# FFN of the second and third token group in triples of hidden units, and one output projection moved ahead

## The chip, the cores and the metric

The kernel runs on one core of one Trainium2 chip. The metric is the device time of one execution in microseconds (us). The engines of the core are named as in the profile: PE is TensorE's matrix multiplication and PEld its weight load, DVE is VectorE, ACT is ScalarE, POOL is GpSimd and SP is SyncE, which here only issues DMAs.

## The reference

The input `x` holds 2048 tokens of 640 values. They are normalized, and two branches work on the result: a local attention with 32 heads of 20 values, in which a token looks at 8 tokens two positions apart, with its own output projection `wo`; and a feed-forward network (FFN) with 1536 hidden values. The branches are multiplied and added to the input.

```
xn  = layernorm(x)
q, k, v = split(xn @ wqkv)                        # 640 -> 3 * 640, 32 heads of 20
s   = local_attention(q, k, v; offsets 0, 2, .. 14) @ wo
g   = silu(silu(xn @ w1) @ w2)                    # 640 -> 1536 -> 640
out = x + s * g
```

## The kernel before

**Groups.** The tokens are worked in four groups of 512: two halves of the sequence, each split by even and odd positions. The texts count them 1 to 4; in the code `g` runs from 0 to 3. A group's 512 tokens are four token tiles (`t`) of 128. Each group passes through a q/k/v stage (`qkv_phase`) and an FFN stage (`ffn_phase`). The attention of a group is computed on VectorE (`scores`, `values`) while TensorE goes on, so a group's output projection (`wo_phase`) comes a stage later: within the FFN stage of the next group. The last group's projection stands at the end (`wo_last`).

**Precision.** Every operand is kept as a high half and a low remainder, and a product is made as high times high, low times high and high times low. So each weight tile (`w`) has a high and a low part, the normalized input has `th` and `tl`, and a hidden unit has `sh` and `sl`.

**FFN units.** The 1536 hidden values are twelve units of 128. *Up* unit f (`up`, L1130 to L1132) makes 15 products of 512 columns into one of two PSUM banks called `rot`. ScalarE then takes silu of the bank twice: once into `sh` (L1143), once into the single buffer `sf` (L1144). VectorE subtracts the two and leaves the low half `sl` (L1145). There are three buffers each of `sh` and `sl`, used in turn. *Down* unit f (`down`, L1003 and L1005 by way of `tm_mm`) makes 16 products from `sh` and then 8 from `sl`, which add into six banks called `acc`: one of 384 columns for each token tile (list `a`) and one of 2 x 256 for each two tiles (list `b`). When all twelve are in, ScalarE takes silu of the sums into `gate` (L1219).

**The output projection.** `wo_phase` has five weight chunks with 24 products each (three for each of four token tiles and two column ranges), L1003 and L1005 again, from `th` and `tl` of the transposed attention output. It takes the same six `acc` banks. VectorE multiplies the sums into `gate` (L1035, six instructions), POOL adds the input (L1049), and SP stores the result. After it `gate` serves as a buffer for transposing the next group's input by DMA (`turn_x`).

**Banks.** `bank()` hands out the six `acc` banks in turn. The q/k/v stage takes four for each of its four quarters, the projection six and the FFN six. ScalarE evacuates the quarters (L733, L736, L739).

**Weights.** All units stand in a list `units` in the order in which TensorE needs them, which is derived from `plan(g)`. A ring of seven buffers `w` is filled seven units ahead: when a unit is done (`w_done`), `w_load` prepares the unit seven places on. Weights that were used before come as ready halves from device memory by a DMA that POOL issues (L564). Fresh ones come raw by a DMA that SP issues (L538), and are split by ScalarE (high half, L573) and VectorE (low half, L577). In group 2 the five chunks of `wo` are fresh, and the FFN units come as ready halves.

**Order.** TensorE's order is the order of the program. For the other engines a planner (`Weave`) lists the instructions with estimated durations and priorities and writes out an order for each queue before the program is built: each engine runs its queue in that order. Every change of TensorE's order therefore lets the planner write new orders for VectorE, ScalarE, POOL and SP. VectorE and POOL instructions marked `lock` are never planned at the same time.

`plan(g)` writes the order of the FFN stage. Before the change it is, for groups 2 to 4: up 0, the projection, and then pairs "up f, up f + 1, down f - 1, down f" (in the last group single units from the seventh on), and the remaining down unit at the end. Group 1 has no projection.

Of the kernel before, what the change touches and what calls it, by code (L numbers as in the profile page):

```python
# [18 lines left out]
DC, FC = D // P, F // P  # L19
# [4 lines left out]
T = 4  # L24
# [5 lines left out]
CA, CB = 384, 256  # L30
RING = 7
NS = 3
SINGLE = 6
RAW_AHEAD = 10
TURNS = 1
FIRST_AT = 44.0, 60.0
# [41 lines left out]
def tsl(t):  # L78
    return slice(t * P, (t + 1) * P)
# [7 lines left out]
class Weave:  # L87
# [22 lines left out]
    def add(self, eng, dur, fn, reads=(), writes=(), prio=0.0, lock=False, table=None, nbytes=0, more=0.0, late=0.0, at=0.0,  # L110
            spans=(), quick=False):
        o = Op()
        o.quick = quick
        o.eng, o.dur, o.fn, o.prio, o.lock, o.table, o.nbytes = eng, dur, fn, prio, lock, table, nbytes
        o.more, o.late, o.spans = more, late, spans
        o.seq, o.users, o.at, o.need = len(self.ops), [], at, 0
        before = set()
        for k in reads:
            if k in self.writer:
                before.add(self.writer[k])  # L120
        for k in writes:
            if k in self.writer:
                before.add(self.writer[k])
            before.update(self.readers.get(k, ()))
        for k in writes:
            self.writer[k] = o
            self.readers[k] = []
        for k in reads:
            self.readers.setdefault(k, []).append(o)
        before.discard(o)  # L130
        self.ops.append(o)
        for b in before:
            self.chain(b, o)
        return o
# [164 lines left out]
def local_attention_silu_ffn(ctx: ExitStack, tc: tile.TileContext, x, wqkv, wo, w1, w2, out):  # L299
# [9 lines left out]
    xg = x.rearrange("b (g p j) d -> (b g) p j d", p=P, j=J)  # L309
    og = out.rearrange("b (g p j) d -> (b g) p j d", p=P, j=J)  # L310
    OL_AT = {10: 2}
    groups = [(h, par) for h in range(2) for par in range(2)]
    NG = len(groups)

    def rows(view, g):
        h, par = groups[g]
        return view[h, :, par::2, :]
# [46 lines left out]
    def take(kind, n):  # L364
        i = count[kind] % n
        count[kind] += 1
        return i

    def bank():
        i = take("acc", 6)  # L370
        return ACC[i], ("acc", i)
# [11 lines left out]
    def dve(n, fn, reads, writes, prio, lock=False, late=0.0, spans=()):  # L383
        return add("DVE", dv(n), fn, reads, writes, prio, lock, late=late, spans=spans)
# [8 lines left out]
    def pe(dur, fn, reads, writes, spans=()):  # L393
        add("PE", dur, fn, reads, writes, spans=spans)
        clock[0] += dur

    def dma(fn, reads, writes, nbytes, prio, dur=0.45, more=0.0, quick=False):
        add("SP", dur, fn, reads, writes, prio, nbytes=nbytes, more=more, quick=quick)
# [15 lines left out]
    def plan(g):  # L414

        last = g == NG - 1
        todo = [("w1", 0)] + [("wo", 0)] * (g > 0)
        down = 0  # L420
        f = 1
        while f < FC:
            k = f // 2
            pair = f + 1 < FC and not (last and f > SINGLE)
            if g < TURNS and 1 <= k <= DC and k - 1 not in X_DMA:
                todo.append(("x", k - 1))
            if last and f in OL_AT:
                todo.append(("o", OL_AT[f]))
            if last and f == FC - 1:
                todo.append(("rest", (0, 1)))  # L430
            n = 2 if pair else 1
            todo += [("w1", u) for u in range(f, f + n)]
            f += n
            todo += [("w2", u) for u in range(down, down + n)]
            down += n
        return todo + [("w2", u) for u in range(down, FC)]

# [2 lines left out]
    for g in range(NG):  # L442
        units += [("q", q, c) for q in range(NQ) for c in range(DC)]
        for kind, f in plan(g):
            units += [("wo", c) for c in range(DC)] if kind == "wo" else [(kind, f)] if kind in ("w1", "w2") else []
# [27 lines left out]
    for u in units:  # L473
        n = seen[u] = seen.get(u, 0) + 1
# [118 lines left out]
    def w_next(*want):  # L593

        i = used[0]
        assert units[i] == want and i < loaded[0], (units[i], want)
        used[0] += 1
        s, n, at = i % RING, width(i), start(i)
        return WR[s][:, at:at + n], WR[s][:, D + at:D + at + n], ("wh", s), ("wl", s)

    def w_done(n=1):
        for _ in range(n):
            w_load()
# [380 lines left out]
    def t_keys(i, cs, ts=range(T), kinds=("th", "tl")):  # L984
        return [(k, i, c, t) for k in kinds for c in cs for t in ts]
# [8 lines left out]
    def tm_banks():  # L994
        a = [bank() for t in range(T)]
        b = [bank() for t in range(T // 2)]
        return a, b

    def tm_mm(banks, t, st, w, first, last, cols=(0, 1)):
        a, b = banks  # L1000
        h = t % 2
        if 0 in cols:
            nc.tensor.matmul(a[t][0][:, :CA], st, w[:, :CA], start=first, stop=last)  # L1003
        if 1 in cols:
            nc.tensor.matmul(b[t // 2][0][:, h * CB:(h + 1) * CB], st, w[:, CA:], start=first and h == 0,  # L1005
                             stop=last, skip_group_check=True)

    def tm_views(banks):

        a, b = banks  # L1010
        for k in range(T // 2):
            for t in (2 * k, 2 * k + 1):
                yield a[t][0][:, :CA].rearrange("p (t m) -> p t m", t=1), a[t][1], slice(t, t + 1), slice(0, CA)
            yield b[k][0].rearrange("p (t m) -> p t m", t=2), b[k][1], slice(2 * k, 2 * k + 2), slice(CA, D)

    def gkeys(ts, cs):
        return [("g", t, cs.start) for t in range(ts.start, ts.stop)]
# [1 line left out]
    TM = mm(CA) + mm(CB)  # L1019

    def wo_phase(g, i):
        banks = tm_banks()
        a, b = banks
        for c in range(DC):
            wh, wl, kh, kl = w_next("wo", c)
            for t in range(T):
                def one(c=c, t=t, wh=wh, wl=wl):
                    tm_mm(banks, t, OH[i][:, c, tsl(t)], wh, c == 0, False)
                    tm_mm(banks, t, OH[i][:, c, tsl(t)], wl, False, False)
                    tm_mm(banks, t, OL[i][:, c, tsl(t)], wh, False, c == DC - 1)  # L1030
                pe(3 * TM, one, t_keys(i, [c], [t]) + [kh, kl], [a[t][1], b[t // 2][1]])
            w_done()
        for p, kp, ts, cs in tm_views(banks):
            n = (ts.stop - ts.start) * (cs.stop - cs.start)
            dve(n, lambda p=p, ts=ts, cs=cs: nc.vector.tensor_tensor(  # L1035
                out=G[:, ts, cs], in0=p, in1=G[:, ts, cs], op=OP.mult), [kp], gkeys(ts, cs), 0, late=ADD_LATE)
        if g == NG - 2:
            for t in range(T):
                xr, kx = (XR[t], [("xr", t)]) if t < 3 else (PRV[:, :D], PRK)
                rest.append((t, xr, kx))  # L1040
                if t < 3:
                    dma(lambda t=t, xr=xr: nc.sync.dma_start(xr, rows(xg, g)[:, t, :]), [], kx, P * D * 4, clock[0] + 5)
            return
        add("DVE", HOLD, lambda: None, [("g", t, CA) for t in range(T)], ["hold"], 0)
        for t in range(T):
            s = take("xr", 3)
            xr = XR[s]
            dma(lambda t=t, xr=xr: nc.sync.dma_start(xr, rows(xg, g)[:, t, :]), [], [("xr", s)], P * D * 4, clock[0] + 5)
            add("POOL", po(D), lambda t=t, xr=xr: nc.gpsimd.tensor_tensor(out=xr, in0=xr, in1=G[:, t, :], op=OP.add),  # L1049
                [("g", t, 0), ("g", t, CA)], [("xr", s)], 500, lock=True)  # L1050
            dma(lambda t=t, xr=xr: nc.sync.dma_start(rows(og, g)[:, t, :], xr), [("xr", s)], [], P * D * 4, clock[0] + 20)
# [208 lines left out]
```

## Time and profile before

| | us |
|---|---|
| three timed runs | 624.53, 624.95, 624.99; median 624.95 |
| the profiled execution | 624.74 |
| its span (first to last instruction) | 623.0 |
| PE busy in it | 617.8 |
| DVE busy in it | 541.4 |
| ACT busy in it | 267.7 |
| POOL busy in it | 114.9 |

The profile shows one execution. Rows of a timeline give the start and the duration in us, then the engine, the line of the kernel, the operation and what it writes and reads; `SPq` is SP's own queue, in which a row is the issue of a DMA and not its transfer. Matmuls are pipelined: each row's duration reaches into the next row, so a block of products is measured from its first start to the first start behind it. A row in brackets at the end tells how long the engine had been idle and what ended that.

### The profile page before, as it was taken

The page shows a single profiled execution, that of the slowest core. Times are in us where ns is not written, and L with a number is a line of the kernel's source. Part 1 is how long each engine was busy: PE and PEld are TensorE (multiplying, and loading weights), DVE is VectorE, ACT ScalarE, POOL GpSimd, SP SyncE. Part 2 cuts the span into 40 slices and gives each one's busy share as a digit, 9 for nine tenths or more (in the row PEclk, how much of TensorE's full clock was granted, in tenths as well). Part 3 has the DMA queues.
Part 4 walks back from the last instruction along what each step waited for, and adds up shares of the span by engine and source line. Part 5 has one row for each costly group of instructions (what it writes and reads, how often), then busy time and mean ns, then how long its engine had stood idle before and what let it go on. Part 6 is the DMA issues. An engine that isn't in the chain of part 4 may idle for free.

```text
span 623.0 us, 9035 instructions
## 1 busy us (share of the span) xinstructions
PE 617.8 (99%) x3403; PEld 558.4 (90%) x3403; DVE 541.4 (87%) x545; ACT 267.7 (43%) x493; POOL 114.9 (18%) x165
## 2 busy tenths in 40 slices
PE   9999999999999999999999999999999999999997
PEld 7888999998889989999888999999988999999997
DVE  7599899999788999899949999989937999898834
ACT  5445555364545224563543604174644353252220
POOL 4800000001110142111221115112222211111100
PEclk9999999999999999999999999999999999999999
DMA  9999999599999989975999999999699999688652
GB/s 296 310 309 318 331 387 375 195 325 267 297 285 317 322 241 319 234 231 139 227 270 258 351 341 304 162 245 355 171 235 270 286 332 269 197 235 246 184 190 86
DMA packets 102873, 166.86 MB, mean 268 GB/s; under 512 B 34365, under 2 KB 64541, under 8 KB 102829
## 3 DMA queue, kind: packets, MB, share of 16 engines
q1 hardware_dynamic: 76333, 86.56, 52.1%
q0 software_dynamic: 25952, 79.31, 45.3%
q8 instruction: 27, 0.44, 0.3%
q10 hardware_dynamic: 544, 0.41, 0.2%
q14 instruction: 17, 0.14, 0.1%
HBM read 107.91 MB, written 34.16 MB: 228 GB/s over the span
## 4 chain that ended last, share of the span: by engine, by line
PE 98%; DMA 0%; DVE 0%; issue 0%
PE acc L1003 22%; PE acc L1005 15%; PE acc L956 10%; PE acc L958 10%; PE acc L957 10%; PE rot L1131 9%; PE rot L1132 9%; PE rot L1130 9%; PE acc L893 2%; PE rot L636 1%; DMA xin<-in_A_x_dram 0%; PE rot L877 0%; PE rot L1116 0%; DVE st L862 0%; PE rot L836 0%; DVE gate L1084 0%
## 5 line engine op out<-in xcount | busy, mean ns | idle before, releaser
L1003 PE MATMUL acc<-w,sh 128*128 128x384 f32 x384 | 113.2, 334 | 0.0
L956 PE MATMUL acc<-w,th 128*128 128x512 f32 (+2 forms) x300 | 113.0, 377 | 0.0
L958 PE MATMUL acc<-w,th 128*128 128x512 f32 (+2 forms) x300 | 112.9, 376 | 0.0
L957 PE MATMUL acc<-w,tl 128*128 128x512 f32 (+2 forms) x300 | 112.8, 376 | 0.0
L776 DVE TENSOR_TENSOR pr<-q,kv 128x2560 f32<-128x2560 f32 x32 | 90.3, 2821 | 22.8 <-DMA kv<-kv 22.6
L1005 PE MATMUL acc<-w,sh 128*128 128x256 f32 x384 | 107.1, 279 | 0.0
L1143 ACT ACTIVATE sh<-rot 128x512 fp32r<-128x512 f32 x48 | 28.8, 599 | 155.4 <-PE rot L1132 155.3
L1130 PE MATMUL rot<-th,w 128*128 128x512 f32 x240 | 94.4, 393 | 0.0
L1132 PE MATMUL rot<-th,w 128*128 128x512 f32 x240 | 93.9, 391 | 0.0
L1131 PE MATMUL rot<-tl,w 128*128 128x512 f32 x240 | 93.8, 391 | 0.0
L810 DVE TENSOR_TENSOR pr<-q,kv 128x2560 f32<-128x2560 f32 x32 | 91.9, 2871 | 0.8
L779 DVE TENSOR_REDUCE l<-pr 128x128 f32<-128x2560 f32 x32 | 89.9, 2810 | 0.2
L564 POOL DMA_DIRECT2D w<-half_q x52 | 37.4, 719 | 234.5 <-DVE pr L815 97.1
L564 POOL DMA_DIRECT2D w<-half_w x72 | 38.9, 541 | 201.7 <-PE acc L1005 86.4
L815 DVE TENSOR_TENSOR pr<-pr 128x1280 f32<-128x1280 f32 x64 | 74.0, 1155 | 1.2
L1005 PEld LDWEIGHTS acc<-w,sh 128*128 128x128 f32 x384 | 72.2, 188 | 1.0
L1003 PEld LDWEIGHTS acc<-w,sh 128*128 128x128 f32 x384 | 72.1, 188 | 1.0
L958 PEld LDWEIGHTS acc<-w,th 128*128 128x128 f32 x300 | 56.3, 188 | 8.8
L956 PEld LDWEIGHTS acc<-w,th 128*128 128x128 f32 x300 | 56.3, 188 | 8.7
L957 PEld LDWEIGHTS acc<-w,tl 128*128 128x128 f32 x300 | 56.3, 188 | 8.7
L733 ACT ACTIVATE kv<-acc 128x320 f32<-128x320 f32 x64 | 28.0, 440 | 75.9 <-PE acc L958 74.5
L1003 PE MATMUL acc<-w,sl 128*128 128x384 f32 x192 | 57.8, 332 | 0.0
(115 smaller groups left out, 1040.3 us busy)
## 6 DMA issues: line engine op xcount, KB each, us to landing
w<-half_w POOLq DMA_DIRECT2D x72, 640.0 KB, 7.3
w<-half_q POOLq DMA_DIRECT2D x39, 512.0 KB, 5.1
half_w<-w SPq DMA_DIRECT2D x24, 640.0 KB
kv<-kv SPq DMA_DIRECT2D x15, 560.0 KB
w<-half_wo POOLq DMA_DIRECT2D x10, 640.0 KB, 6.9
kv<-kv SPq DMA_DIRECT2D x15, 420.0 KB
gate<-in_B_w_dram SPq DMA_DIRECT2D x16, 320.0 KB
w<-half_q POOLq DMA_DIRECT2D x13, 384.0 KB, 7.4
```

Source lines behind the costliest of these rows:

```text
L564: add("POOL", 1.0, lambda: nc.gpsimd.dma_start(both, src), [("half", u), ("half", u, "more")], [kh, kl], due + 10, nbytes=2 * n * P * 4)
L776: dve(2560, lambda t=t: nc.vector.tensor_tensor(out=PR, in0=win(qq[:, t:t + 2, :], W, 0), in1=win(kv[:, 0, t:t + 2, :], W, CQ), op=OP.mult ...
L779: dve(2560, lambda t=t: nc.vector.tensor_reduce(out=l[:, t:t + 2].rearrange("p t w h -> p (t w h)"), in_=PR.rearrange("p t w (h d) -> p (t ...
L810: dve(2560, lambda t=t, v=v: nc.vector.tensor_tensor(out=PR.rearrange("p t w (h d) -> p t (w h) d", d=DH), in0=e[:, t:t + 2].rearrange("p ...
L956: nc.tensor.matmul(o, hi, wh, start=c == 0, stop=False)
L957: nc.tensor.matmul(o, lo, wh, start=False, stop=False)
L958: nc.tensor.matmul(o, hi, wl, start=False, stop=c == DC - 1)
L1003: nc.tensor.matmul(a[t][0][:, :CA], st, w[:, :CA], start=first, stop=last)
L1005: nc.tensor.matmul(b[t // 2][0][:, h * CB:(h + 1) * CB], st, w[:, CA:], start=first and h == 0, stop=last, skip_group_check=True)
L1130: nc.tensor.matmul(h, wh[:, cs], TH[i][:, c, :], start=c == 0, stop=False)
L1131: nc.tensor.matmul(h, wh[:, cs], TL[i][:, c, :], start=False, stop=False)
L1132: nc.tensor.matmul(h, wl[:, cs], TH[i][:, c, :], start=False, stop=c == DC - 1)
```

## The change

`plan(g)` no longer works out the order by a rule, but reads it from a table `STEPS` with one row per group. A row is a list of steps, each with up units and the down units that follow them. Groups 1 and 4 have the order they had. Groups 2 and 3 go up three units and down the same three. Group 3 keeps up 0 and then the projection ahead of its first full step, which has two up units; group 2 begins with the projection, and its first step has up units 0, 1 and 2.

The second edit concerns all three calls of `wo_phase`: it still takes six banks in turn, but gives them to the sums in another order. The list `b` (256-column sums) gets the first and the fifth, the list `a` (384-column sums) the second, third, fourth and sixth.

```diff
-SINGLE = 6
...
+    STEPS = [
+        (((0,), ()), ((1, 2), (0, 1)), ((3, 4), (2, 3)), ((5, 6), (4, 5)), ((7, 8), (6, 7)), ((9, 10), (8, 9)), ((11,), (10, 11))),
+        (((0, 1, 2), (0, 1, 2)), ((3, 4, 5), (3, 4, 5)), ((6, 7, 8), (6, 7, 8)), ((9, 10, 11), (9, 10, 11))),
+        (((0,), ()), ((1, 2), (0, 1, 2)), ((3, 4, 5), (3, 4, 5)), ((6, 7, 8), (6, 7, 8)), ((9, 10, 11), (9, 10, 11))),
+        (((0,), ()), ((1, 2), (0, 1)), ((3, 4), (2, 3)), ((5, 6), (4, 5)), ((7,), (6,)), ((8,), (7,)), ((9,), (8,)), ((10,), (9,)), ((11,), (10, 11))),
+    ]
...
-        todo = [("w1", 0)] + [("wo", 0)] * (g > 0)
-        down = 0
-        f = 1
-        while f < FC:
-            k = f // 2
-            pair = f + 1 < FC and not (last and f > SINGLE)
+        todo = [("wo", 0)] * (g > 0 and len(STEPS[g][0][1]) > 0)
+        k = 0
+        for ups, downs in STEPS[g]:
...
-            n = 2 if pair else 1
-            todo += [("w1", u) for u in range(f, f + n)]
-            f += n
-            todo += [("w2", u) for u in range(down, down + n)]
-            down += n
-        return todo + [("w2", u) for u in range(down, FC)]
+            todo += [("w1", f) for f in ups] + [("w2", f) for f in downs]
+            if not downs:
+                todo += [("wo", 0)] * (g > 0)
+            else:
+                k += 1
+        return todo
...
     def wo_phase(g, i):
-        banks = tm_banks()
+        n = [bank() for t in range(T + T // 2)]
+        banks = [n[1], n[2], n[3], n[5]], [n[0], n[4]]
```

More of the change, by code (lines that the diff above doesn't have):

```diff
@@ L418, in plan @@
         last = g == NG - 1
-        todo = [("w1", 0)] + [("wo", 0)] * (g > 0)
-        down = 0
-        f = 1
-        while f < FC:
-            k = f // 2
-            pair = f + 1 < FC and not (last and f > SINGLE)
+        todo = [("wo", 0)] * (g > 0 and len(STEPS[g][0][1]) > 0)
+        k = 0
+        for ups, downs in STEPS[g]:
             if g < TURNS and 1 <= k <= DC and k - 1 not in X_DMA:
                 todo.append(("x", k - 1))
-            if last and f in OL_AT:
-                todo.append(("o", OL_AT[f]))
-            if last and f == FC - 1:
+            if last and ups[0] in OL_AT:
+                todo.append(("o", OL_AT[ups[0]]))
+            if last and ups[0] == FC - 1:
                 todo.append(("rest", (0, 1)))
-            n = 2 if pair else 1
-            todo += [("w1", u) for u in range(f, f + n)]
-            f += n
-            todo += [("w2", u) for u in range(down, down + n)]
-            down += n
-        return todo + [("w2", u) for u in range(down, FC)]
+            todo += [("w1", f) for f in ups] + [("w2", f) for f in downs]
[4 more added lines that the diff above has]
+        return todo
     units = []
```

## The prediction

> **What bounds the kernel now.** I read the page first: the sums, the slices and the chain that ended last.
>
> ```profile
> span 623.0 us, 9035 instructions
> PE 617.8 (99%) x3403; PEld 558.4 (90%) x3403; DVE 541.4 (87%) x545; ACT 267.7 (43%) x493; POOL 114.9 (18%) x165
> PE   9999999999999999999999999999999999999997
> PEclk9999999999999999999999999999999999999999
> PE 98%; DMA 0%; DVE 0%; issue 0%
> ```
>
> TensorE is busy all the way at the full granted clock, and the chain of waits is 98% TensorE. VectorE has 87%. So a change of order can gain only what one order of the same products costs more than another, and it loses wherever it makes TensorE wait. The profiled execution took 624.74 us, 1.74 more than its span; the three timed runs have their median at 624.95, 0.21 above it. Differences found below are subtracted from that median. A measurement of this kernel can tell about 0.2%, 1.25 us, from no change.
>
> Next the timeline of TensorE at the edges of its blocks: the first up units of group 1 (g = 0 in the code), group 2's blocks (g = 1), then group 3's (g = 2). L1130 is an up unit, L1003 from `th` the output projection, from `sh` a down unit. The first two columns are start and duration.
>
> ```profile
> 60.88 0.39 PE L1130 MATMUL rot<-th,w 128*128 128x512 f32 x1
> ...
> 71.11 0.34 PE L1003 MATMUL acc<-w,sh 128*128 128x384 f32 x1
> ...
> 197.16 0.49 PE L1130 MATMUL rot<-th,w 128*128 128x512 f32 x1
> ...
> 200.71 0.34 PE L1003 MATMUL acc<-w,th 128*128 128x384 f32 x1
> ...
> 217.92 0.40 PE L1130 MATMUL rot<-th,w 128*128 128x512 f32 x1
> ...
> 224.77 0.34 PE L1003 MATMUL acc<-w,sh 128*128 128x384 f32 x1
> ...
> 231.66 0.40 PE L1130 MATMUL rot<-th,w 128*128 128x512 f32 x1
> ...
> 286.62 0.40 PE L1130 MATMUL rot<-th,w 128*128 128x512 f32 x1
> ...
> 290.07 0.34 PE L1003 MATMUL acc<-w,sh 128*128 128x384 f32 x1
> ...
> 349.03 0.48 PE L1130 MATMUL rot<-th,w 128*128 128x512 f32 x1
> ...
> 352.57 0.34 PE L1003 MATMUL acc<-w,th 128*128 128x384 f32 x1
> ...
> 376.63 0.34 PE L1003 MATMUL acc<-w,sh 128*128 128x384 f32 x1
> ```
>
> From one edge to the next: two up units 224.77 - 217.92 = 6.85; one alone 290.07 - 286.62 = 3.45; so a second unit behind a first costs 3.40, and the first of a row 0.05 more. Two down units take 231.66 - 224.77 = 6.89, 3.445 each. The output projection takes 217.92 - 200.71 = 17.21, 3.44 for each of its five weight chunks and 0.86 for a token tile of one. Three up units already stand in a row in group 1: 71.11 - 60.88 = 10.23.
>
> **The sum: fewer first units.** No product, load or evacuation is added or removed; groups 1 and 4 keep their order. In group 2 the ups cost 3.55 (behind transposes) + 5 x 6.85 + 3.45 = 41.25 now. Four triples of 3.45 + 2 x 3.40 = 10.25 are 41.00: 0.25 less. The 0.10 by which the unit behind the transposes exceeds 3.45 passes to the projection, which now stands there: between 0, if shorter products take it up, and 0.10; I take 0.10, since it is the same four transposes. Group 2 gains 0.15. Group 3 keeps its first unit and the projection: 3.54 + 34.25 + 3.45 = 41.24 becomes 3.54 + 6.85 + 3 x 10.25 = 41.14, a gain of 0.10. The twelve downs are 41.34 in both orders. Sum **-0.25**; with group 1's 10.23 for each of the seven triples and no price for the transposes it would be -0.49. So 624.95 - 0.25 = 624.70.
>
> **What must still be hidden.** With triples a unit's product is wanted as late as now: after up f come two ups, or up and down, or two downs. The silu copies leave a bank as follows (ScalarE, group 2, behind the up unit that ended at 221.37 and its successor).
>
> ```profile
> 221.57 0.60 ACT L1143 ACTIVATE sh<-rot 128x512 fp32r<-128x512 f32 x1 [14.94 <-PE rot L1132]
> 222.06 0.59 ACT L1144 ACTIVATE sf<-rot 128x512 f32<-128x512 f32 x1
> ```
>
> The bank is free at 222.65. The third unit of a triple wants it 3.40 after 221.37, at 224.77: cover 2.12, cost nothing; it is gone where the second copy first waits longer than that for VectorE's subtraction before, and each us beyond is then one of TensorE. The three `sh` buffers are refilled only after three downs, so they add no wait.
>
> **The projection ahead of group 2's first unit** moves the projection 3.45 earlier: its start passes from 200.71 to 197.26 (197.16 and the 0.10). Three things must now be there sooner: the evacuated banks, five weight chunks, and behind it VectorE's six multiplications. These rows stand around that place.
>
> ```profile
> 197.94 0.43 ACT L733 ACTIVATE kv<-acc 128x320 f32<-128x320 f32 x1
> 198.26 0.23 ACT L736 ACTIVATE q<-acc 128x64 f32<-128x64 f32 x1
> 198.36 0.75 ACT L573 ACTIVATE w<-xr 128x640 fp32r<-128x640 f32 x1
> ...
> 202.48 0.60 ACT L1143 ACTIVATE sh<-rot 128x512 fp32r<-128x512 f32 x1
> ...
> 204.64 1.98 ACT L573 ACTIVATE w<-xr 128x640 fp32r<-128x640 f32 x3
> ...
> 199.14 0.82 DVE L577 TENSOR_TENSOR w<-xr,w 128x640 fp32r<-128x640 f32 x1
> ...
> 205.40 1.56 DVE L577 TENSOR_TENSOR w<-xr,w 128x640 fp32r<-128x640 f32 x2 [0.87 <-ACT w L573]
> 206.88 2.82 DVE L776 TENSOR_TENSOR pr<-q,kv 128x2560 f32<-128x2560 f32 x1
> ...
> 212.47 0.81 DVE L577 TENSOR_TENSOR w<-xr,w 128x640 fp32r<-128x640 f32 x1
> ...
> 193.07 0.83 SPq L538 DMA_DIRECT2D xr<-in_A_wo_dram  x2
> ...
> 200.09 1.49 SPq L538 DMA_DIRECT2D xr<-in_A_wo_dram  x1
> ...
> 184.29 0.56 POOL L564 DMA_DIRECT2D w<-half_w  x1 [3.05 <-DMA half_q<-w]
> ```
>
> Banks: the last evacuation ends at 198.49. In the new order of banks only the fourth token tile writes that bank, at 197.26 + 3 x 0.86 = 199.84: cover 1.35, cost nothing.
>
> Weights: chunks start at 197.26, 200.70, 204.14, 207.59 and 211.03, and a low half is first used 0.29 later (one pair of products, 17.21 / 60). The second chunk's is ready at 199.96, 1.0 early. The third's is ready at 206.22 (the first of two from 205.40), the fifth's at 213.28: **both too late by the present order**, the third by 206.22 - 204.43 = 1.79. They need not stand there: the loads of chunks three and four were issued at 193.07, and between its copies at 198.36 and 204.64 ScalarE took the silu of the up unit (202.48) that now comes later. The two ends are 0, if the kernel's planner puts the splits ahead, and 1.79 with a remainder for the fifth chunk (211.32 + 1.79 = 213.11 against 213.28), 1.96 in all. I take 0, since the free time lies in these rows. The fifth chunk's load was issued at 200.09 and had landed by its ScalarE copy, the last of three that ended at 206.62, so by 205.87. The load of the first up unit's weights (640 KB, POOL at 184.29) passes behind five slots, into this stretch; the DMA moved 321 GB/s there (the next fence), so 655,360 bytes put the landing back by up to 2.04. Landed by 207.91, copied in 0.75, subtracted in 0.82, it is there at 209.48, 1.84 before 211.32. One score product of 2.82 in between would use that up.
>
> ```profile
> 200.71:217.92 17.21, 17.21 (x121) 17.21 (x120) 15.95 (x15) 5.76 (x9) 2.65 (x5) 1.00 1.06 321
> ```
>
> SP's other work here (halo copies, x loads and stores of the projection) keeps its order or moves 3.45 earlier with the projection; the transposing DMAs for the next group's x follow the projection and gain that time. The multiplications now have three ups (10.25) before the first down, instead of two.
>
> **Group 3 and VectorE.** Here the first triple comes right behind the projection's additions on POOL.
>
> ```profile
> 373.80 1.59 POOL L1049 TENSOR_TENSOR xr<-xr,gate 128x640 f32<-128x640 f32 x1
> ...
> 375.90 1.58 POOL L1049 TENSOR_TENSOR xr<-xr,gate 128x640 f32<-128x640 f32 x1
> ...
> 378.53 1.60 POOL L1049 TENSOR_TENSOR xr<-xr,gate 128x640 f32<-128x640 f32 x1
> ...
> 371.85 3.14 DVE L1035 TENSOR_TENSOR gate<-acc,gate 128x384 f32<-128x384 f32 x6
> 374.90 5.79 DVE L1145 TENSOR_TENSOR sl<-sf,sh 128x512 fp32r<-128x512 f32 x1
> ...
> 382.59 0.67 DVE L1145 TENSOR_TENSOR sl<-sf,sh 128x512 fp32r<-128x512 f32 x1
> ```
>
> The new bank order makes the first down (376.63) write what the last of the six multiplications reads: done at 374.99, cover 1.64. A multiplication started one score product later would cost 1.18.
>
> The low half of unit 1 took 5.79 us beside the three additions and ended at 380.69. Unit 2's ended at 383.26. Now an up pair follows down 1; with triples down 2 does, at 376.63 + 6.89 = 383.52, and its low-half products come 8 x 0.287 = 2.30 later, at 385.82. Its cover shrinks to 2.56. I take 0 for it; the other end is below.
>
> The Trainium skill (SBUF — State Buffer, "SBUF: two separate sides") says that GpSimd's and a two-input VectorE operation hold their shared ports as a lock, each for one whole instruction. By that rule the subtraction would have run when the first addition ended, at 375.39, and have ended 4.6 us sooner; unit 2's, behind it, would have that much more room and rival (b) would be empty. The trace disagrees: the subtraction outlasted three additions and the gaps between them, so the measured 5.79 decides.
>
> **The rivals.**
> (a) *The third chunk's low half comes late in group 2.* For it: the splits stand just in time in the rows above, at the end of ScalarE's and VectorE's queues, and behind a busy DMA. Against it: the free stretch on ScalarE. Price 1.96, 624.70 + 1.96 = 626.66, **slower**; it decides from a low half that ends after 204.43.
> (b) *VectorE does not keep pace with three subtractions in a row in group 3.* For it: 2.56 us of cover, less than one score product of 2.82; a product ahead of unit 2's subtraction makes it 0.26 late, and with a fourth addition of 1.59 in the burst 1.85. Against it: the other triples come without additions. 624.70 + 1.85 = 626.55, slower.
> (c) *The dearer first unit does not depend on its predecessor* but on something that triples don't remove. Then nothing is saved: 624.95. Against it: the triple in group 1 at 10.23.
> (d) *More is gained than first units.* TensorE would have to lose over 1.25 us of idleness that the page does not show; at 0.05 that is 25 first units, and only five are removed. About 623.5.
>
> **How the numbers follow.** Forecast 0.50 (its own range 624.4 to 625.3); (a) 0.24; (b) 0.16; (c) 0.06; (d) 0.04. Forecast and (c) are no change at 0.2%: 0.56; (a) and (b) slower: 0.40; (d) faster: 0.04. The range goes down to 624.2 (-0.49 and the runs' own scatter) and up to 627.8, past (a) and (b) alone and half of what both together (628.5) would add.
>
> **What would show it.** TensorE's timeline in groups 2 and 3: triples of 10.23 to 10.25 and downs of 10.3 between them, each start on the end before. Wrong would be: a gap within the projection of group 2, with VectorE's L577 ending at it (rival a); a gap ahead of the `sl` products of a triple's third down, with L1145 ending at it (b); triples of 10.35 (c); a gap anywhere else, in the projection's first tiles (banks) or at the start of the next group's q/k/v products, which I have not priced. A span above 624.3 us proves the forecast wrong, one between 622.4 and 623.0 bears it out.

## The result, and the profile after

| 22 runs each, in turn | median | lowest | highest |
|---|---|---|---|
| before | 624.94 us | 624.53 | 625.79 |
| after | 626.67 us | 625.41 | 633.61 |

The ratio is 1.0047, interval 1.0026 to 1.0069; it goes by the means, which the long executions pull up (628.0 against 625.0). At the median the change costs 1.73 us, where the prediction had a gain of 0.25. Two things come together. The best execution is 0.88 us worse, and the executions scatter: 8 of the 22 runs after took over 627 us, none of the 22 before. (Of the runs over 635 further below, one of e1 and two of e2 are slow ones and stand outside the ratios.)

The profiled execution after took 625.41 us. Its page begins as follows.

```profile
span 623.6 us, 9036 instructions
PE 618.2 (99%) x3403; PEld 559.0 (90%) x3403; DVE 539.6 (87%) x545; ACT 269.2 (43%) x494; POOL 116.6 (19%) x165
PE   9999999999999999999999999999999999999997
PEclk9999999999999999999999999999999999999999
```

This is one of the short executions, with no wait of TensorE in groups 2 and 3. It shows the first loss alone. In TensorE's timeline these are the edges in groups 2 and 3 (L1005 is now the projection and the down units, L1133 an up unit, L958 the q/k/v stage):

```profile
197.10 0.43 PE L1005 MATMUL acc<-w,th 128*128 128x384 f32 x1
...
215.16 0.40 PE L1133 MATMUL rot<-th,w 128*128 128x512 f32 x1
...
225.37 0.34 PE L1005 MATMUL acc<-w,sh 128*128 128x384 f32 x1
...
235.70 0.40 PE L1133 MATMUL rot<-th,w 128*128 128x512 f32 x1
...
245.94 0.34 PE L1005 MATMUL acc<-w,sh 128*128 128x384 f32 x1
...
297.44 0.40 PE L958 MATMUL acc<-w,th 128*128 128x512 f32 x1
...
449.18 0.40 PE L958 MATMUL acc<-w,th 128*128 128x512 f32 x1
```

The next q/k/v stages of the kernel before began here:

```profile
296.96 0.40 PE L956 MATMUL acc<-w,th 128*128 128x512 f32 x1
...
448.82 0.40 PE L956 MATMUL acc<-w,th 128*128 128x512 f32 x1
```

Three ups take 225.37 - 215.16 = 10.21 and 245.94 - 235.70 = 10.24, three downs 10.33. But the projection takes 215.16 - 197.10 = **18.06** instead of 17.21. From the first product behind its q/k/v stage to the next group's q/k/v, group 2 took 296.96 - 197.16 = 99.80 before and takes 297.44 - 197.10 = 100.34 now: 0.54 more. Group 3, its q/k/v stage included, took 448.82 - 296.96 = 151.86 and takes 449.18 - 297.44 = 151.74: 0.12 less. The span is 0.6 longer in all: 0.36 of it stands at the last products (618.90 against 618.54), the rest lies behind them and is not explained.

The same five chunks of 24 products, in the same execution, once in group 2 and once in group 3. The columns of the view by stretches are the busy time and count of PE, PEld, DVE, ACT and POOL, then the granted clock, the DMA share and GB/s.

```profile
197.10:215.15 18.05, 18.05 (x123) 18.05 (x122) 16.46 (x20) 8.55 (x12) 3.53 (x6) 1.00 1.14 309
...
353.05:370.26 17.21, 17.21 (x122) 17.21 (x120) 16.97 (x16) 4.84 (x7) 2.12 (x4) 1.00 1.09 357
```

No product waits and the clock is 1.00 in both: each pair of a 384-column and a 256-column product takes 18.05 / 60 = 0.301 us in group 2, and 17.21 / 60 = 0.287 in group 3.

A later execution of the same kernel, 630.33 us, shows the second loss. What TensorE waited for in groups 2 and 3 (total, count and longest):

```profile
PE rot L1133 <- ACT sf L1147: 3.0, 1, 3.0
...
PE rot L1133 <- DMA w<-half_w: 0.9, 1, 0.9
```

Neither is in the short execution: up units wait for a bank that ScalarE has not emptied, and for their half weights. (At the kernel's start every trace has a wait of 1.4 us for POOL, and some have a further one, of up to 1.2, for the first normalized input.) The chain of waits ahead of the 3.0, for that stretch:

```profile
254.38 4.01 SPq L674
258.39 0.04 issue
258.44 24.30 DMA gate<-gate
...
282.82 1.38 ACT xin L683
...
284.22 0.63 ACT th L687
...
284.85 1.28 ACT L1146
...
286.15 0.60 ACT sh L1146
286.75 0.50 ACT sf L1147
```

A transposing DMA of x (`gate<-gate`) came late; ScalarE, which works its queue in order, stood idle for 8.71 us at the copy that joins its halves (L683), and the silu copies stood behind that. SP's queue in the same execution, and then in the profiled one before, tells how long the issues of the same transposes took (6.25 in the short execution of the kernel after):

```profile
253.95 21.57 SPq L674 DMA_TRANSPOSE gate<-gate  x4
```

```profile
256.44 5.89 SPq L672 DMA_TRANSPOSE gate<-gate  x4
```

### The profile page after: what moved, and what is told of

Its sections match the earlier page's. It is cut to its first block, busy times and chain, and to the rows that moved or that the text cites. A ratio compares the mean times of both kernels' runs of the same rounds, so it can differ in the third digit from the quotient of the medians.

```text
span 623.6 us, 9036 instructions
## 1 busy us (share of the span) xinstructions
PE 618.2 (99%) x3403; PEld 559.0 (90%) x3403; DVE 539.6 (87%) x545; ACT 269.2 (43%) x494; POOL 116.6 (19%) x165
## 4 chain that ended last, share of the span: by engine, by line
PE 98%; DMA 0%; DVE 0%; issue 0%
PE acc L1005 22%; PE acc L1007 15%; PE acc L958 10%; PE acc L959 10%; PE acc L960 10%; PE rot L1134 9%; PE rot L1135 9%; PE rot L1133 9%; PE acc L895 2%; PE rot L638 1%; DMA xin<-in_A_x_dram 0%; PE rot L879 0%; PE rot L1119 0%; DVE st L864 0%; PE rot L838 0%; DVE gate L1087 0%
## 5 line engine op out<-in xcount | busy, mean ns | idle before, releaser
L1005 PE MATMUL acc<-w,sh 128*128 128x384 f32 x384 | 113.1, 333 | 0.0
L958 PE MATMUL acc<-w,th 128*128 128x512 f32 (+2 forms) x300 | 113.0, 377 | 0.0
L1133 PE MATMUL rot<-th,w 128*128 128x512 f32 x240 | 94.3, 393 | 0.0
L817 DVE TENSOR_TENSOR pr<-pr 128x1280 f32<-128x1280 f32 x64 | 75.5, 1180 | 1.4
L1005 PEld LDWEIGHTS acc<-w,sh 128*128 128x128 f32 x384 | 72.1, 188 | 0.9
L958 PEld LDWEIGHTS acc<-w,th 128*128 128x128 f32 x300 | 56.3, 188 | 8.7
L1005 PE MATMUL acc<-w,sl 128*128 128x384 f32 x192 | 57.8, 332 | 0.0
```

What stands on the lines that cost most here:

```text
L958: nc.tensor.matmul(o, hi, wh, start=c == 0, stop=False)
L1133: nc.tensor.matmul(h, wh[:, cs], TH[i][:, c, :], start=c == 0, stop=False)
```

## The experiments

Fifteen runs. The times of the kernel before were taken again on the chip of each batch: medians 624.99, 625.14, 624.96 and 625.00. Letters of theories hold within a batch; D means something else in the first one than in the last two.

**First batch: the two parts alone.** `e1_triples_only` has the triples without the moved projection, since group 2 gets group 3's row:

```diff
-        (((0, 1, 2), (0, 1, 2)), ((3, 4, 5), (3, 4, 5)), ...
+        (((0,), ()), ((1, 2), (0, 1, 2)), ((3, 4, 5), (3, 4, 5)), ...
```

> Group 2 keeps its first up unit ahead of the projection, as group 3 does; the triples and the new bank order stay. Theory M (the loss is the projection that now stands directly behind the q/k/v stage of group 2): the projection is back at 17.21 us, the time is 0.2 to 0.3 below the kernel before, about 624.7, and no execution lies above 626. Theory T (the loss is the triples, whose subtractions VectorE doesn't finish in time): the time stays near 626.7, with executions up to 633.

Measured: median 626.67, lowest 624.51, highest 636.29, ratio 1.0031 (1.0005 to 1.0058); 4 of 12 runs over 627. The projection is back to 17.21 (200.97:218.18 below), and the lowest run to the level of before; the scatter stays. So theory M explains the slower projection, not the long executions.

`e2_projection_only` has the moved projection and one triple behind it, and pairs from there on and in group 3:

```diff
+        (((0, 1, 2), (0, 1)), ((3, 4), (2, 3)), ..., ((11,), (10, 11))),
+        (((0,), ()), ((1, 2), (0, 1)), ((3, 4), (2, 3)), ..., ((11,), (10, 11))),
```

> Pairs as before the change in groups 2 and 3, but the projection of group 2 directly behind its q/k/v stage (then three ups, two downs, and pairs); new bank order. Theory M: the projection takes 18.05 us as in the changed kernel, the lowest executions lie some 0.8 above the kernel before, and some executions reach 629 to 633. Theory T: the projection's cadence may be slow, but no execution lies above 627.

Measured: 626.48, lowest 625.88, highest 636.57, ratio 1.0030 (1.0015 to 1.0045). The projection takes 18.06, and 5 of 12 runs are over 627. So the slower projection belongs to the move alone, but the scatter appears with either part. Both runs keep the new order of banks, and no run has that order alone: as a cause of the scatter it is untested.

`e4_transposes_earlier` tests whether the four transposes on TensorE, which stand just ahead of the projection, slow it. It puts them two weight chunks (24 products) earlier in the last q/k/v quarter:

```diff
-... {(2, 4): (2, 3), (3, 4): (4,)}),
+... {(2, 4): (2, 3), (3, 2): (4,)}),
```

> The changed kernel, with the four transposes of the fifth chunk of group 2's attention output moved from behind the last q/k/v weight chunk to behind the third one of the last quarter. Theory C (four transposes directly ahead put the projection in a slower cadence of 0.300 us for a pair of products instead of 0.287, which it doesn't leave): the projection takes 17.2 us and the lowest executions lie at or below the kernel before, about 624.6. Theory D (the cadence is slow because the projection stands where it does, beside the work of VectorE, ScalarE and the DMAs there): it stays at 18.05. Neither says that the executions of 629 to 633 go away.

Measured: 626.66, ratio 1.0042 (1.0017 to 1.0066), 5 of 12 runs over 627. The projections of e4 and of e1, side by side:

```profile
197.26:215.26 18.00, 18.00 (x122) 18.00 (x121) 17.65 (x24) 8.27 (x13) 3.54 (x6) 1.00 1.17 301
```

```profile
200.97:218.18 17.21, 17.21 (x121) 17.21 (x120) 15.94 (x15) 5.87 (x9) 2.64 (x5) 1.00 1.12 323
```

With q/k/v products directly ahead it is slow too, so the transposes are not the cause; what e1 has ahead of its projection is an up unit.

`after_again` is the kernel after, once more, for its trace:

> The changed kernel once more, for a second profile. If this execution is one of the long ones (over 627), theory M expects a gap of TensorE in group 2's projection, at its third to fifth weight chunk, with a raw load of that chunk landing late; theory T expects it ahead of a triple's low-half products. If it is a short one, the projection takes 18.05 again (theory C and D alike) and nothing is told of the long ones.

Measured: 625.80, the projection 18.05 again, no wait in groups 2 and 3.

**What a long execution looks like.** The profiled execution of e1 took 633.80. What TensorE waited for, and SP's transposes in group 3, there and in the kernel before:

```profile
PE rot L1133 <- DMA w<-half_w: 3.0, 1, 3.0
PE acc L958 <- ACT gate L1222: 2.1, 1, 2.1
```

```profile
408.78 2.61 SPq L674 DMA_TRANSPOSE gate<-turn  x2
411.43 26.77 SPq L674 DMA_TRANSPOSE gate<-gate  x4
```

```profile
408.74 3.17 SPq L672 DMA_TRANSPOSE gate<-turn  x2
411.95 12.12 SPq L672 DMA_TRANSPOSE gate<-gate  x4
```

Four transposes took 26.77 us to issue instead of 12.12, and the loads of half weights issued at that time came late as well (their landings stand below). The wait of 2.1, at the start of the next q/k/v products, has the same chain as the one of `after_third`: ScalarE's joining copy (L683) starts at 450.47, after 4.00 us of idling for a transposing DMA of x, and the silu copies into `gate` (L1222) stand behind it; TensorE goes on at 456.10.

**Second batch: one place in POOL's queue.** In e1's group 3 one weight load stands ahead of POOL's fourth addition, which in the kernel before holds the loads back until 419. `e5_swap_back` is e1 with that load put back behind the addition, `e7_after_swap_back` the kernel after with the same, `e6_swap_in_before` the kernel before with one load ahead of the addition:

```diff
+            if u == ("w1", 9) and units[:i].count(u) == 2:
+                wv.chain(fourth[0], o)
```

```diff
+            if u == ("w1", 10) and units[:i].count(u) == 2:
+                wv.chain(o, fourth[0])
```

> e1_triples_only with one weight load of group 3 (the half weights of up unit 9) put back behind POOL's fourth addition, where that kernel's POOL queue had it ahead; all else is in the same order but for two neighbours on VectorE. Theory V (the load ahead of the addition goes out while the transposing DMAs of the next group's x run, and the loads after it come too late for TensorE in some executions): 624.6 to 624.9 in the median, 0.1 to 0.4 below the kernel before, and no execution above 626.5. Theory T (the triples themselves need the weights in a burst that the DMAs don't deliver): the median stays near 626.7 with a third of the executions above 627.

> The kernel before, with its pairs and its bank order, and on POOL the one swap the other way: in group 3 the half weights of up unit 10 are loaded ahead of the fourth addition instead of behind it. Theory V: the time spreads out as with the changed kernel, a median of 625.5 to 627 and some executions above 628. Theory T: 624.9 to 625.1, as before.

> The changed kernel with the same swap back as in e5. Theory V: the long executions are gone and what is left is the projection's slower cadence (0.84 us) less the triples' gain: a median of 625.3 to 625.7, at most 626.5. If long executions stay, the moved projection has a late transfer of its own in group 2. Theory T: as the changed kernel, 626.7.

> The changed kernel for a further profile. Theory V: if it is a long one (over 627), TensorE's gap stands in group 3's last up triple or at the start of group 4's q/k/v products, behind half weights that landed some 20 us after their issue. Theory M (the projection's weights in group 2): the gap stands in group 2's projection. A short one tells nothing.

Measured: e5 625.16, ratio 1.0026 (1.0002 to 1.0050), with 3 of 12 runs still at 630 to 631.5. e6 624.98, ratio 0.9995 (0.9987 to 1.0004), none over 627. e7 627.33, ratio 1.0041 (1.0017 to 1.0065), 8 of 11 over 627. `after_third`, 630.33, is the long execution shown with the result. The swap alone makes no long executions in the kernel before and cures none in the kernel after: theory V falls.

**Third batch: without the transposes, bunched ones, and wide products.** `e9_no_transposes` takes away the transposing DMAs of x in groups 2 and 3 and keeps every queue's order.

```diff
-            dma(lambda h=h: nc.sync.dma_start_transpose(
+            dma(lambda h=h: turn and nc.sync.dma_start_transpose(
...
-        join(to, XIN[:, :, c * P:(c + 1) * P], ...
+        join((by[0], to[1]), XIN[:, :, c * P:(c + 1) * P], ...
```

> The kernel after, without the twenty DMAs that transpose x for groups 3 and 4 (five chunks of two in each of groups 2 and 3); ScalarE's joining copies read the chunk as it was sent, so x is not transposed there. Every queue keeps its order and every other instruction. Theory D (the long executions, up to 636 us, arise where these transposes and the loads of half weights share the DMA engines): all runs lie within 0.7 us of the fastest, median 625.4 to 625.9, ratio about 1.001, which is the projection's slower cadence alone; the loads in groups 2 and 3 land within 10 us. Theory L (the long executions come from the order of TensorE and the queues, or from the loads among themselves): at least three of twelve runs above 627, as in the kernel after.

Measured: four runs, 625.61 to 625.72, ratio 1.0011 (0.9999 to 1.0024). The last batch has eleven more.

`e10_bunched_before` is the kernel before with the last three chunks of x in group 2 sent in a row (a send is a copy on ScalarE and two transposing DMAs behind it).

```diff
+        if i == 0 and c >= 2:
+            wv.chain(chunk[-1], o)
+            chunk.append(o)
```

> The kernel before, in group 2 alone with the last three chunks of x sent to their transposes one behind the other, after the second chunk was joined, as it stands in the kernel after: six transposes in a row in place of two and, some 4 us later, four. Theory B (a row of six transposes is what starts the slow transfers): at least three of twelve runs above 627 us, median above 625.5. Against B: the order of the sends is no matter, median as before, 624.9 to 625.2.

Measured: 626.63, 626.07, 625.39 and 625.22, ratio 1.0014 (1.0001 to 1.0027). The median rose to 625.73, but none is over 627, and the waits in its trace lie elsewhere, at 446 in group 3, whose orders the edit moved too. There the late transposes show without triples and without the moved projection: four took 21.91 us to issue, ScalarE stood idle for 4.88 and 3.97 at joining copies, and TensorE waited 0.8 for the silu copy behind the second. On theory B four runs decide nothing.

`e12_wide_first` puts five products of 512 columns ahead of group 2's projection.

```diff
+            if g == 0 and c == 0:
+                h, kp = rot()
+                for k in range(WIDE):
+                    pe(mm(TOK), lambda h=h, wh=wh: nc.tensor.matmul(h, wh[:, tsl(0)], OH[i][:, 0, :], start=True, stop=True), ...
```

> The kernel after with five products of 512 columns, whose result nobody reads, ahead of group 2's projection. Theory C (the projection runs at 0.300 us per pair behind the q/k/v products, since no product of 512 columns has gone before, which gives the weight loads their lead): 17.21 us for the projection, and with 5 x 0.228 = 1.14 for the added products 0.30 above the kernel after in short executions, 625.7 at the fastest. Theory P (the slower cadence belongs to the place, something else that runs then): 18.05 us as in the kernel after, 1.14 above it, 626.5 at the fastest.

```profile
197.53 1.40 PE L1033 MATMUL rot<-th,w 128*128 128x512 f32 x5
198.77 0.34 PE L1006 MATMUL acc<-w,th 128*128 128x384 f32 x1
...
215.97 0.40 PE L1138 MATMUL rot<-th,w 128*128 128x512 f32 x1
```

The projection takes 215.97 - 198.77 = **17.20**: the place is not at fault, and five wide products ahead restore the cadence, as theory C has it. They gain nothing, since they take 198.77 - 197.53 = 1.24 themselves. That they do it by a lead for the weight loads, theory C's reason, is not shown. The runs (626.34 to 632.52) lie above the 625.7 expected; the profiled one, 628.52, has a wait of 2.0 for half weights.

**Last batch: the parts without the transposes.** `e15_before_no_transposes`, `e13_triples_no_transposes` and `e9_again` are the kernels before, e1 and after with e9's edit; `e16_one_wide` is e9 with `WIDE = 1`.

> The kernel before without the same twenty DMAs; every queue keeps its order. The base for e9 and e13: 624.5 to 624.9 in all runs. Theory D: e9 above it by 0.84 - 0.25 = 0.6 us, e13 below it by 0.2. Theory L: below 624.3, if the transposes cost TensorE time in the kernel before as well.

> The kernel of e1_triples_only (group 2 keeps up 0 and then the projection, as group 3; triples in both) without the twenty DMAs that transpose x for groups 3 and 4, so x is not transposed there. Theory D (the triples' long executions come from these transposes beside the loads of half weights; what is left is their gain): no run above 626, all within 0.5 us, and 0.2 us below the kernel before without the same transposes (e15). Theory L (the triples make TensorE wait for other reasons too): some runs above 627.

> The kernel of e9_no_transposes once more, beside its base e15 on the same chip. Theory D: all runs within 0.3 us, 625.5 to 625.9, 0.6 above e15. Theory L: runs above 627 among them, as in 7 of 22 of the kernel after above 629.

> The kernel after without the same twenty DMAs (e9), with one product of 512 columns, whose result nobody reads, ahead of group 2's projection. Theory C (one wide product gives the weight loads their lead): projection 17.21 us, 0.23 - 0.84 = 0.6 below e9, so 625.0 to 625.1. Against it (five were needed): 18.05 us as in e9, and 0.2 above it.

| eleven runs each | median | lowest | highest | ratio to before |
|---|---|---|---|---|
| e15, before | 625.21 | 624.95 | 626.14 | 1.0005 (0.9995 to 1.0014) |
| e13, triples only | 624.85 | 624.52 | 625.50 | 0.9995 (0.9986 to 1.0003) |
| e9_again, after | 625.56 | 625.43 | 626.23 | 1.0006 (0.9998 to 1.0015) |
| e16, after and one wide product | 625.81 | 625.37 | 626.73 | 1.0014 (1.0005 to 1.0023) |

No run of the four kernels, nor of e9's first four, took over 626.8; with the transposes, 4 of 12 runs of e1 and 8 of 22 of the kernel after were over 627. So the long executions need the transposes, as theory D has it. The edit takes away their traffic, their issues on SP and ScalarE's waits for them all at once, so it does not tell which of these is to blame. The projection takes 18.06 in e9's trace too: its slower cadence does not come from these transposes. Triples alone are 0.36 below e15 and the kernel after 0.35 above it, both in the expected direction (8 of e13's 11 runs lie at or below e15's lowest); the intervals of the ratios overlap, so these two sizes are only indicated (0.2 and 0.6 had been expected). The scatter without transposes is wider than expected, up to 1.4 us. One wide product does not restore the cadence: e16's projection took 17.99.

```profile
197.31:215.30 17.99, 17.99 (x121) 17.99 (x120) 16.46 (x21) 8.52 (x12) 3.04 (x6) 1.00 1.05 321
```

What the transposes do to the loads, from the DMA view of the stretch from 375 to 450 us, the packets, the queue that holds SP's transfers (packets, MB, share of the engines' time) and the loads of half weights (count, size, median time to landing). The kernel before:

```profile
DMA packets 10832, 18.91 MB, mean 252 GB/s; under 512 B 5961, under 2 KB 5969, under 8 KB 10827
...
q1 hardware_dynamic: 6616, 3.97, 39.7%
...
w<-half_w POOLq DMA_DIRECT2D x17, 640.0 KB, 9.4
```

e1's long execution:

```profile
DMA packets 9654, 16.59 MB, mean 221 GB/s; under 512 B 5873, under 2 KB 5879, under 8 KB 9649
...
w<-half_w POOLq DMA_DIRECT2D x17, 640.0 KB, 15.6
```

And e15, the kernel before without these transposes:

```profile
DMA packets 5311, 17.20 MB, mean 229 GB/s; under 512 B 520, under 2 KB 528, under 8 KB 5305
...
q1 hardware_dynamic: 1172, 2.65, 9.7%
...
w<-half_w POOLq DMA_DIRECT2D x16, 640.0 KB, 5.5
```

Ten transposes are about 5961 - 520 = 5441 packets under 512 bytes, half of all packets. With them a load of half weights lands after 9.4 us, in the long execution after 15.6, and without them after 5.5. The kernel after has 9.1 and, as e9_again, 4.7. That is group 3; in group 2, from 225 to 300 us, the landing is about the same with the transposes (5.2 in the kernel before) and without (5.0 in e15), and it rises only where they are slow (15.1 in `after_third`). The Trainium skill (DMA: Bandwidth & Descriptors, "Specifications") puts the least transfer that runs at line rate at 512 bytes; the rows agree in so far as SP's queue takes 39.7 - 9.7 = 30.0% of the engines' time more for 1.32 MB more, but all these small packets are transposes as well, and the rows don't part the two.

## Why the prediction was wrong, point by point

**The sum of first units held.** Forecast were four triples of 10.25 and a gain of 0.10 in group 3; measured are 10.21 to 10.25 and 0.12, and the downs are 10.33. Rival (c), triples of 10.35, is out.

**The projection's price is the first step that failed.** It was moved at its old length, with the 0.10 of the unit behind the transposes, which "passes to the projection". That took 17.21 to be the price of these products wherever they stand. It is their price behind an up unit: the move made it 18.06, a loss of 0.85 in place of 0.10. Group 2 follows: 0.85 for the projection, ups 40.94 instead of 41.25, downs 41.34 as before, so +0.54 instead of -0.15. With group 3's -0.12 this is +0.42 in an execution without waits. The trace of before had the warning in it: it held no projection behind q/k/v products, so the step needed a bound, and 0 to 0.10 was too narrow. Shown are that it comes with the move (e1 against e2), that neither the four transposes on TensorE (e4) nor the transposing DMAs (e9) are the cause, and that five wide products restore it and one does not (e12, e16). Why 512-column products do this is not shown.

**Costing the covers at nothing is the second.** The prediction had the transposing DMAs for the next group's x "follow the projection and gain that time", and named only the start of the q/k/v products and the projection's first tiles as places it had not priced. It priced neither the landing of half weights for the triples nor ScalarE's wait for the joined x ahead of the silu copies. Nor did it price the start of the q/k/v products, which it named; e1's long execution waited 2.1 there. Without the transposes the kernel after is 0.56 above the kernel before on the same chip (e9_again, 625.56 against 625.00), so some 1.2 of the 1.73 goes with them. The long traces show what these microseconds are: the waits, and the lower clock behind some of them. No execution at the median was traced, so how the 1.2 divides among them there is not shown. The cover of the third unit of a triple, 2.12, was "gone where the second copy first waits"; in the long execution the copies did wait, but for a late transpose ahead of them in ScalarE's queue and not for VectorE's subtraction.

**The rivals.** The measured median lies inside the stated range, 624.2 to 627.8, but by luck: its upper part was made for rivals (a) and (b). Rival (a) gives nearly the measured median, 626.66, by a mechanism that did not occur: VectorE's low half for the third chunk is done by 203.25, ahead of 204.43, those for the last two by 205.83, and there is no gap in the projection.

```profile
202.43 0.82 DVE L579 TENSOR_TENSOR w<-xr,w 128x640 fp32r<-128x640 f32 x1
204.27 1.56 DVE L579 TENSOR_TENSOR w<-xr,w 128x640 fp32r<-128x640 f32 x2
```

Rival (b) did not occur either. In group 3 the subtraction that took 5.79 us before takes 0.69 in the profiled execution after. VectorE's subtractions and POOL's additions there:

```profile
375.03 0.69 DVE L1148 TENSOR_TENSOR sl<-sf,sh 128x512 fp32r<-128x512 f32 x1 [0.19 <-ACT sf L1147]
...
378.42 0.69 DVE L1148 TENSOR_TENSOR sl<-sf,sh 128x512 fp32r<-128x512 f32 x1 [0.73 <-ACT sf L1147]
```

```profile
375.97 2.58 POOL L1052 TENSOR_TENSOR xr<-xr,gate 128x640 f32<-128x640 f32 x1
...
379.09 1.60 POOL L1052 TENSOR_TENSOR xr<-xr,gate 128x640 f32<-128x640 f32 x1
```

The first subtraction ended at 375.72, 0.25 ahead of the first addition, and the second began 0.13 before that addition ended, at 378.55. This differs from one execution to the next: in `after_again`, the same kernel, the second subtraction took 4.64 us beside the additions, and in e1, with triples in group 3 as well, the first took 6.03. TensorE waited for none of them, so the cover that the prediction left held.

**What stays open.** Without the transposes the long executions are gone, but the kernel before has the same twenty transposes and rarely a long execution: none of 22 beside the kernel after, 6 of the 103 in the four batches over 627. With either part of the change, and the new bank order in both, they become frequent. The one swap in POOL's queue does not account for it (e6); for the row of sends four runs are too few (e10), and the bank order was not run alone. An order of the sends that keeps transposes and loads apart was not run either. What makes the long executions frequent stays open.

## What to carry to other kernels

A block's measured length holds for the block that stands ahead of it; where a block is moved behind another kind, bound its cadence from the trace and don't carry the old length over. A kernel whose engine is 99% busy can live on the slack of its DMAs: list, for each transfer that shares the DMA engines, its time to landing against its lead, and treat a queue entry that waits for a DMA ahead of a silu copy as part of TensorE's path. Where runs scatter, take the trace of a long one; its waits name what no short one shows.

## What the hardware showed unasked

**The clock after a wait.** In e1's long execution TensorE stands for 3.04 us up to 434.92. About a microsecond later its 512-column products go at half speed for 3 us: starts 0.43 apart, where 0.23 is usual.

```profile
434.92 0.47 PE L1133 MATMUL rot<-th,w 128*128 128x512 f32 x1 [3.04 <-DMA w<-half_w]
...
435.95 0.63 PE L1134 MATMUL rot<-tl,w 128*128 128x512 f32 x1
436.38 0.63 PE L1135 MATMUL rot<-th,w 128*128 128x512 f32 x1
...
439.32 0.40 PE L1133 MATMUL rot<-th,w 128*128 128x512 f32 x1
```

The wait of 2.1 us at the next q/k/v stage was followed by a granted clock of 0.53; the wait of 3.0 in the kernel after's long execution by 1.00:

```profile
456.10:459.50 3.40, 3.40 (x9) 2.64 (x9) 3.37 (x3) 3.40 (x7) 0.00 (x0) 0.53 0.53 166
```

```profile
287.29:290.70 3.41, 3.41 (x15) 2.83 (x16) 3.41 (x3) 0.41 (x1) 0.09 (x1) 1.00 0.96 217
```

The Trainium skill (TensorE: Matmul & The Clock Gate, "What's actually happening") has the clock halved after at least one idle window of about 3.4 us. Here a wait of 2.1 was enough once, and one of 3.0 was not in another execution; so the length of a wait alone did not decide. The lower clock is no small part of a long execution: e1's took 633.80 - 624.51 = 9.3 us more than its shortest, its two waits are 5.1, and its mean granted clock of 0.993 over 631.9 us is, as an estimate, another 4.4.
